# Six tiles of three blocks in a second network, and a last expert in ranges of 384 and 256 rows

## The chip, the core and the metric

The kernel runs on one core of one Trainium2 chip. Times are device microseconds (us) of one execution. The clock of TensorE, as the profile grants it, has two levels here, 2.4 and 1.2 GHz. Engines are named as in the profile: PE is TensorE (PEld its weight loads), DVE VectorE, ACT ScalarE, POOL GpSimd, SP SyncE; a q behind a name is the engine's DMA queue.

## The reference, cut to what matters

Windowed attention gives 2304 rows of 512; each row goes to two of eight experts (512 to 1024 to 512), and the weighted sum of their two answers goes through a second network (512 to 2048 to 512).

```python
x = attention(q, k, v)                                   # 2304 x 512
...
for e in range(8):                                       # each row has two experts
    h = np.maximum(x[mask] @ w1[e], 0.0)
    out[mask] += top2_w[mask, k, None] * (h @ w2[e])
...
h = x @ w_in                                             # 512 -> 2048
g = h * np.clip(h + 3.0, 0.0, 6.0) / 6.0
return g @ w_out                                         # 2048 -> 512
```

## The kernel before

Every product is made of three matmuls in a reduced 32-bit type: weights and rows are each split into a high and a low half (names beginning with h and l), and high by high, high by low, low by high are summed in PSUM.

**The experts.** Each expert has room for five blocks of 128 rows (`CAP`). It works in two ranges. For experts 1 to 7 each range takes 320 rows in its first product (`expert_sub`, lines 898 to 912): eight f blocks, each 12 matmuls with the rows as the moving operand, then a ReLU on ScalarE into `hh` and the low half on VectorE into `hl`. An f block's sum lies in one of four PSUM tiles in turn (three `ph`, one `ph4`), so f block 4 takes the tile that `hl` of f block 0 reads last. The second product (lines 913 to 933) makes the output blocks m, 24 matmuls of 512 columns each: m 0 and 1 behind the first range, m 2 to 4 behind the second. ScalarE copies a block to `y` and stores it in the DRAM tensor `y_rows`.

**The second network.** Its 18 blocks of 128 rows come in tiles (`TILES`, line 944). To begin a tile, each of its blocks is gathered from `y_rows` by eight indirect DMAs of GpSimd into two tiles `xg` (`fetch`), combined with the gates on ScalarE and VectorE, four instructions each (`combine`), and transposed and split into `xh` and `xl` (`tokens`). A gather of block i of tile 0 has to wait for block i of every expert, the last one's too. A tile does two halves, each with eight f blocks of 12 matmuls, whose moving width is the tile's rows (256 for two blocks, 384 for three), and 24 matmuls of 512 columns for each block of rows.

**What sets the order.** From the experts on, every engine runs its instructions in the order in which the code is written. Side work is hung into the loops by keys: `put(f, "f", 3, 0)` runs f inside f block 3 (ahead of its ReLU), `("f", 3, 1)` behind it, `("m", 2, 1)` inside output block 2. Beside the gathers these are the steps that fetch and split the second network's weights: a copy of the high half on ScalarE (line 589), the low half on VectorE (line 595), through two buffers `wraw`. Before the change tile 0's two blocks are gathered in the last expert's second range and combined behind its f blocks, at its output blocks 2 and 3.

Of the kernel before, what the change touches and what calls it, by code (L numbers as in the profile page):

```python
# [21 lines left out]
E = 8  # L22
# [7 lines left out]
CAP = 5  # L30
LIM = CAP * 128
SUBS = ((0, 2), (2, CAP))

HOLD = SUBS[0][1] * 128
KNOWN = 2

# [9 lines left out]
def attention_moe_kernel(ctx, tc, q, k, v, w_gate, w_noise, noise, w1, w2, w_in, w_out, out):  # L46
# [459 lines left out]
    XG, XT2 = {}, {}  # L506
# [31 lines left out]
    def turn_rows(src, hi, lo, c0):  # L538

        tr = ps.tile([128, 4, 128], F32, name="tr", bufs=2)  # L540
        for a in range(4):
            pe.transpose(tr[:, a], src[:, a * 128:(a + 1) * 128], ident)
        halves(tr, hi, lo, c0)

    def columns(e, s):
        if (e, s) not in XT2:
            XT2[e, s] = [(ep if s else mp).tile([128, 4, 384], F32R, name=f"{nm}{s}") for nm in ("xh", "xl")]
        return XT2[e, s]

    def build(e, m):  # L550
        if e == 0:
            s = int(m >= SUBS[0][1])
            turn_rows(XG[e, m], *columns(e, s), 128 * (m - SUBS[s][0]))
        elif m == 2:

            turn(XG[e, m], (*columns(e, 0), 0), (*columns(e, 1), 0))
        else:
            s = int(m > 2)
            turn(XG[e, m], (*columns(e, s), 64 + 128 * (m - 3 * s)))
# [319 lines left out]

    def expert_sub(e, s, at):  # L880

        m0, m1 = SUBS[s]


        if e == 0:
            n, c0, b0 = 128 * (m1 - m0), 0, 0
        else:
            n, c0, b0 = 64 * CAP, 64 * s, 64 - 64 * s
        xh, xl = XT2[e, s]
        if e == 0 or s == 0:  # L890
            HH[:] = [[ep.tile([128, 384], F32R, name=f"{nm}{f}") for f in range(8)] for nm in ("hh", "hl")]
        hh, hl = HH

        def also(*key):
            for f in at.get(key, ()):
                f()

        for f in range(8):
            p = sums()[:, :n]
            fs = slice(128 * f, 128 * f + 128)  # L900
            for d in range(4):
                wh, wl = W["w1", e, d]
                pe.matmul(p, wh[:, fs], xh[:, d, :n], start=(d == 0), stop=False)  # L903
                pe.matmul(p, wh[:, fs], xl[:, d, :n], start=False, stop=False)  # L904
                pe.matmul(p, wl[:, fs], xh[:, d, :n], start=False, stop=(d == 3))  # L905
                if d == 1:
                    also("f", f, 0)
                also("d", f, d)
            cs = slice(c0, c0 + n)
            act.activation(hh[f][:, cs], p, AF.Relu)  # L910
            dve.scalar_tensor_tensor(hl[f][:, cs], p, 0.0, hh[f].bitcast(F32)[:, cs], op0=OP.max, op1=OP.subtract)  # L911
            also("f", f, 1)
        for m in range(m0, m1):
            also("m", m, 0)
            ms = slice(b0 + 128 * (m - m0), b0 + 128 * (m - m0) + 128)
            if e and m % 3 == 2:
                p = ps.tile([128, DM], F32, name="tr", bufs=2)
            else:
                p = eps.tile([128, DM], F32, name="py", bufs=2)
            for f in range(8):  # L920
                wh, wl = W["w2", e, f // 2]
                ws = slice(512 * (f % 2), 512 * (f % 2) + 512)
                pe.matmul(p, hh[f][:, ms], wh[:, ws], start=(f == 0), stop=False)  # L923
                pe.matmul(p, hh[f][:, ms], wl[:, ws], start=False, stop=False)  # L924
                pe.matmul(p, hl[f][:, ms], wh[:, ws], start=False, stop=(f == 7))  # L925
                if f in (2, 5):
                    also("m", m, 1 + f // 3)
                also("s", m, f)
            also("m", m, 3)
            y = ep.tile([128, DM], F32, name="y")  # L930
            act.copy(y.rearrange("q (a k y) -> q k a y", a=4, k=4), p.rearrange("q (k a y) -> q k a y", a=4, k=4))  # L931
            r = (m * E + e) * 128
            act.dma_start(ybuf[r:r + 128], y)
# [7 lines left out]
               [Narrow(w_out, w_out32, c) for c in range(PER // CH)], 2)  # L941
    A1, M = SUBS[0][1], CAP

    TILES = (2, 3, 3, 3, 3, 2, 2)
    BASES = [sum(TILES[:t]) for t in range(len(TILES))]
    TT = 128 * max(TILES)
    NF = F2 // 128
# [26 lines left out]
    for e in range(E):  # L974
        at = {}

        def put(f, *key):
            at.setdefault(key, []).append(f)
# [27 lines left out]
        if 0 < e < 5:  # L1006
            for f in range(8):
                put(lambda: next(table, None), "f", f, 1)
        expert_sub(e, 0, at)

        at.clear()
# [14 lines left out]
        if e + 1 < E:  # L1026
            for m, f, late in ((0, 0, ("f", 6, 0)), (1, 2, ("m", A1, 1)), (2, 4, ("m", A1 + 1, 0))):
                put(lambda m=m: gather(e + 1, m), "f", f, 0)
                put(lambda m=m: build(e + 1, m), *late)
            if e == 0:  # L1030
                for key in (("f", 1, 1), ("f", 3, 0), ("f", 4, 1), ("f", 6, 1), ("m", A1, 1), ("m", A1, 3),
                            ("m", A1 + 1, 2), ("m", A1 + 2, 1)):
                    put(wq.settle, *key)
            for key in ((("f", 1, 0), ("f", 2, 1), ("f", 4, 0), ("f", 5, 1), ("f", 7, 1), ("m", A1, 2),
                         ("m", A1 + 1, 1), ("m", A1 + 1, 3)) if e == 0 else
                        (("f", 1, 1), ("f", 5, 0), ("m", A1, 0), ("m", A1 + 1, 1), ("m", A1 + 2, 0))):
                put(wq.step, *key)
            if e:
                for key in (("f", 0, 1), ("f", 2, 1), ("f", 4, 1), ("m", A1, 2), ("m", A1 + 1, 2), ("m", A1 + 2, 2)):
                    put(nq.step, *key)  # L1040
        else:
            while nq.at < len(nq.items):
                nq.step()
            store_narrow()
            narrow.close()
            wpool[2] = pool_of(ctx, "w2")
            fp = pool_of(ctx, "ffn")
            for f in (1, 3, 6):
                put(wq.step, "f", f, 1)
            for i in range(2):  # L1050
                put(lambda i=i: fetch(0, i), "f", 3 * i, 0)
                put(lambda i=i: combine(0, i), "m", A1 + i, i)
                put(lambda i=i: tokens(0, i), "m", A1 + i, 1 + i)
            for key in (("m", A1, 2), ("m", A1 + 1, 0), ("m", A1 + 2, 0), ("m", A1 + 2, 2)):
                put(wq.step, *key)
            for key in (("f", 2, 1), ("f", 4, 1), ("f", 7, 1), ("m", A1, 3), ("m", A1 + 1, 3), ("m", A1 + 2, 1), ("m", A1 + 2, 3)):
                put(wq.settle, *key)
            put(lambda: fetch(1, 0), "m", A1 + 2, 0)
        expert_sub(e, 1, at)
        store_narrow()  # L1060

# [100 lines left out]
    for t, ni in enumerate(TILES):  # L1162
# [9 lines left out]

        if t + 1 < len(TILES):

            put(lambda: fetch(t + 1, 1), "f", 2)
            put(lambda: combine(t + 1, 0), 0, 0, 3)
            put(lambda: tokens(t + 1, 0), 0, 1, 0)
            if TILES[t + 1] > 2:
                put(lambda: fetch(t + 1, 2), 0, 1, 1)
            put(lambda: combine(t + 1, 1), 0, 1, 3)  # L1180
            put(lambda: tokens(t + 1, 1), 1, 0, 0)
            if TILES[t + 1] > 2:
                put(lambda: combine(t + 1, 2), 1, 0, 3)
                put(lambda: tokens(t + 1, 2), 1, 1, 0)
            if 0 < t < len(TILES) - 2:
                put(lambda: fetch(t + 2, 0), 1, 1, 3)
        if t == 0:
            for key in (("f", 2), ("f", 6), (0, 0, 1), (0, 0, 6)):
# [5 lines left out]
        for half in range(2):  # L1194
# [18 lines left out]
            for i in range(ni):  # L1213
                if t + 1 == len(TILES) and half == 1 and i == 1:
                    e = mybir.EngineType
                    tc.mark_branch_hint_location("over", "LikelyTaken", engines=[e.PE, e.DVE, e.SP])
                ms = slice(128 * i, 128 * i + 128)
                if half == 0:
                    py[i] = eps.tile([128, DM], F32, name="py", bufs=2) if i < 2 else ps.tile([128, DM], F32, name="tr", bufs=2)
                for f in fs:  # L1220
                    wh, wl = W["w_out", f // 2]
                    ws = slice(512 * (f % 2), 512 * (f % 2) + 512)
                    pe.matmul(py[i], gh[f][:, ms], wh[:, ws], start=(f == 0), stop=False)  # L1223
                    pe.matmul(py[i], gh[f][:, ms], wl[:, ws], start=False, stop=False)  # L1224
                    pe.matmul(py[i], gl[f][:, ms], wh[:, ws], start=False, stop=(f == NF - 1))  # L1225
                    also(half, i, f % 8)
                if half == 1:

                    if t == 0 and i == 1:
                        fetch(2, 0)  # L1230
                    store(py[i], 128 * (BASES[t] + i))
    overflow()

# [31 lines left out]
```

## Time and profile before

| | us |
|---|---|
| median of 3 runs | 1007.03 |
| lowest, highest | 1004.6, 1007.49 |
| the profiled execution's own time | 1009.37 |
| its span, first to last instruction | 1007.6 |
| TensorE busy in it | 983.8 |
| VectorE, ScalarE, GpSimd busy | 573.9, 467.8, 324.7 |

The span is what the trace covers; 1.8 us of the profiled execution's time lie around it. TensorE's matmuls are pipelined: a row's duration is longer than the spacing of two rows, and the spacing is what a matmul costs in a row of them.

### The profile page before, as it was taken

What the parts mean: (1) busy time and instruction counts of PE and PEld (TensorE: products, weight loads), DVE (VectorE), ACT (ScalarE), POOL (GpSimd) and SP (SyncE); (2) the same over time, 40 slices, a digit from 0 to 9 for tenths busy, and PEclk for the clock granted to TensorE, in tenths of its full rate; (3) what the DMA queues carried; (4) which work ended last, traced back from release to release, by engine and by line L of the source; (5) the groups of instructions that cost most, each with busy time, mean ns of one, the idle gap of its engine ahead of it and who ended that gap; (6) DMA issues with size and microseconds to landing.
All of it is one profiled execution on the core that took longest, in us unless ns stands there. A gap on an engine that the chain in (4) does not pass through costs nothing.

```text
span 1007.6 us, 17479 instructions
## 1 busy us (share of the span) xinstructions
PE 983.8 (98%) x6392; PEld 893.7 (89%) x6392; DVE 573.9 (57%) x1550; ACT 467.8 (46%) x1032; POOL 324.7 (32%) x351
## 2 busy tenths in 40 slices
PE   8989898999999999999999999999999999999998
PEld 7979886999897999999998988989988998899997
DVE  6687975556777776666667656444333433344322
ACT  6867651444544454444454546434333433334333
POOL 2122202732535334242431276732343234410000
PEclk9999998999999999999999999999999999999999
DMA  9897441546656666656666454200111002000000
GB/s 168 169 221 190 119 147 50 165 139 201 214 163 197 192 184 193 186 186 209 215 195 196 151 191 133 70 23 19 58 32 46 24 26 63 27 27 22 11 11 23
DMA packets 116395, 122.43 MB, mean 122 GB/s; under 512 B 69840, under 2 KB 78288, under 8 KB 116304
## 3 DMA queue, kind: packets, MB, share of 16 engines
q1 hardware_dynamic: 96144, 86.17, 31.0%
q0 software_dynamic: 9488, 19.94, 7.1%
q10 hardware_dynamic: 10672, 15.15, 4.1%
q8 instruction: 51, 0.84, 0.3%
q14 instruction: 40, 0.33, 0.1%
HBM read 92.91 MB, written 28.31 MB: 120 GB/s over the span
## 4 chain that ended last, share of the span: by engine, by line
PE 80%; DVE 9%; DMA 5%; ACT 3%; issue 2%; POOL 0%; ACTq 0%; DVEq 0%; SPq 0%
PE ph L1204 6%; PE ph L1202 6%; PE ph L1203 6%; PE ph L903 6%; PE ph L904 6%; PE ph L905 6%; PE py L1225 5%; PE py L1224 5%; PE py L1223 5%; PE py L923 4%; PE py L924 4%; PE py L925 4%; PE s L242 3%; PE pv L295 2%; PE tr L1225 1%
## 5 line engine op out<-in xcount | busy, mean ns | idle before, releaser
L522 POOL DMA_INDIRECT xg<-x_rows,idx x140 | 145.1, 1037 | 221.2 <-DVE xt L533 169.8
L959 POOL DMA_INDIRECT xg<-y_rows,rows x144 | 144.3, 1002 | 222.4 <-DVE xg L967 74.5
L1207 DVE SCALAR_TENSOR_TENSOR g<-g,ph 128x384 f32<-128x384 f32 (+1 forms) x112 | 55.7, 497 | 158.8 <-ACT g L1206 154.5
L1206 ACT ACTIVATE g<-ph,three 128x384 f32<-128x384 f32 (+1 forms) x112 | 60.0, 536 | 100.7 <-PE ph L1204 97.7
L911 DVE SCALAR_TENSOR_TENSOR hl<-ph,hh 128x320 fp32r<-128x320 f32 (+2 forms) x128 | 61.0, 487 | 74.1 <-ACT hh L910 74.1
L1212 DVE TENSOR_TENSOR hl<-g,hh 128x384 fp32r<-128x384 f32 (+1 forms) x112 | 56.2, 502 | 58.9 <-ACT hh L1210 56.1
L910 ACT ACTIVATE hh<-ph 128x320 fp32r<-128x320 f32 (+2 forms) x128 | 54.6, 436 | 65.2 <-PE ph L905 61.2
L1210 ACT CAST hh<-g 128x384 fp32r<-128x384 f32 (+1 forms) x112 | 52.4, 467 | 63.8 <-DVE g L1207 63.8
L527 ACT CAST xh<-xt 128x512 fp32r<-128x512 f32 (+1 forms) x60 | 33.6, 570 | 81.9 <-DVE xt L533 81.2
L528 DVE TENSOR_TENSOR xl<-xt,xh 128x512 fp32r<-128x512 f32 (+1 forms) x60 | 37.2, 630 | 39.7 <-ACT xh L527 39.7
L242 PE MATMUL s<-kt,qbd 128*128 128x128 f32 x288 | 43.7, 293 | 0.2 <-ACT kt L227 0.2
L242 PEld LDWEIGHTS s<-kt,qbd 128*128 128x128 f32 x288 | 40.2, 207 | 0.6 <-ACT kt L227 0.5
L157 POOL TENSOR_SCALAR vt<-vt 64x520 f32<-64x520 f32 (+1 forms) x32 | 19.3, 604 | 57.0 <-DMA vt<-in_v_dram 53.2
L533 DVE STREAM_TRANSPOSE xt<-xg 128x512 f32<-128x512 f32 x53 | 37.4, 706 | 0.4
L762 DVE SCALAR_TENSOR_TENSOR na<-mag,raw 128x256 f32<-128x256 f32 x64 | 26.9, 420 | 12.7 <-DMA w_out<-na 5.1
L759 ACT ACTIVATE mag<-raw 128x256 f32<-128x256 f32 x64 | 27.6, 431 | 12.6 <-DVE na L768 12.6
L257 ACT ACTIVATE pb<-sm,mx 128x128 f32<-128x128 f32 x90 | 30.0, 397 | 5.8 <-DVE mx L250 5.7
L768 DVE CUSTOM_DVE_ANT_0 na<-mag,nr 128x512 uint16<-128x512 uint16 x64 | 27.3, 426 | 9.5 <-DVE mag L767 0.5
L931 ACT COPY y<-py 128x512 f32<-128x512 f32 x33 | 19.3, 584 | 27.1 <-PE py L925 14.1
L270 ACT COPY ptb<-pt 128x384 f32<-128x384 f32 x48 | 23.1, 480 | 12.7 <-PE pt L265 10.7
L767 DVE SCALAR_TENSOR_TENSOR mag<-na,mag 128x256 int32<-128x256 int32 x64 | 27.2, 425 | 2.2
L295 PE MATMUL pv<-vt,ptb 128*64 128x65 f32 x640 | 26.1, 226 | 1.8 <-DVE xbuf L314 1.8
(520 smaller groups left out, 3201.7 us busy)
## 6 DMA issues: line engine op xcount, KB each, us to landing
wraw<-in_moe_w_dram SPq DMA_DIRECT2D x60, 512.0 KB, 4.6
y_rows<-y ACTq DMA_DIRECT2D x40, 256.0 KB, 3.4
raw<-in_moe_w_in_dram SPq DMA_DIRECT2D x32, 256.0 KB, 3.8
raw<-in_moe_w_out_dram SPq DMA_DIRECT2D x32, 256.0 KB, 3.0
rq<-in_q_dram SPq DMA_DIRECT2D x32, 144.0 KB, 3.7
rk<-in_k_dram SPq DMA_DIRECT2D x32, 144.0 KB, 2.9
x_rows<-xbuf SPq DMA_DIRECT2D x18, 256.0 KB
out_dram<-y ACTq DMA_DIRECT2D x17, 256.0 KB, 2.2
```

The costliest lines, as they stand in the source:

```text
L242: pe.matmul(s[:, i, :], l, KT[n][:, k0:k0 + 128], start=(g in LIGHT), stop=(g in LIGHT or i == 2))
L522: pool.indirect_dma_start(out=t[:, i], out_offset=None, in_=pieces(xrows), in_offset=bass.IndirectOffsetOnAxis(ap=idx4[:, i, e, m:m + 1], ...
L903: pe.matmul(p, wh[:, fs], xh[:, d, :n], start=(d == 0), stop=False)
L904: pe.matmul(p, wh[:, fs], xl[:, d, :n], start=False, stop=False)
L905: pe.matmul(p, wl[:, fs], xh[:, d, :n], start=False, stop=(d == 3))
L911: dve.scalar_tensor_tensor(hl[f][:, cs], p, 0.0, hh[f].bitcast(F32)[:, cs], op0=OP.max, op1=OP.subtract)
L959: pool.indirect_dma_start(out=g[:, r], out_offset=None, in_=pieces(left), in_offset=bass.IndirectOffsetOnAxis(ap=rows4[:, r, tt, j:j + 1], ...
L1202: pe.matmul(p, wh[:, c], xh[:, d, :n], start=(d == 0), stop=False)
L1203: pe.matmul(p, wh[:, c], xl[:, d, :n], start=False, stop=False)
L1204: pe.matmul(p, wl[:, c], xh[:, d, :n], start=False, stop=(d == 3))
L1206: act.activation(g, p, AF.Relu, bias=three)
L1225: pe.matmul(py[i], gl[f][:, ms], wh[:, ws], start=False, stop=(f == NF - 1))
```

## The change

The second network takes six tiles of three blocks instead of tiles of 2, 3, 3, 3, 3, 2 and 2. So that tile 0's third block can be gathered, the last expert's ranges become 384 rows (blocks 0 to 2, the third one whole) and 256 rows (blocks 3 and 4), its `hh` and `hl` are new tiles in its second range, and output block 2 is made behind the first range. Gathers, combines and weight steps get new places.

```diff
+LAST = ((0, 3), (3, CAP))
...
+        elif e + 1 == E:
+            s = int(m >= LAST[0][1])
+            turn(XG[e, m], (*columns(e, s), 128 * (m - LAST[s][0])))
...
-        m0, m1 = SUBS[s]
...
-        if e == 0:
+        m0, m1 = (LAST if e + 1 == E else SUBS)[s]
...
+        if e in (0, E - 1):
             n, c0, b0 = 128 * (m1 - m0), 0, 0
...
-    TILES = (2, 3, 3, 3, 3, 2, 2)
+    TILES = (3,) * 6
...
+        if e + 1 == E:
+            put(lambda: fetch(0, 0), "m", 1, 2)
+            put(lambda: fetch(0, 1), "m", 2, 2)
         expert_sub(e, 0, at)
...
-            for i in range(2):
-                put(lambda i=i: fetch(0, i), "f", 3 * i, 0)
-                put(lambda i=i: combine(0, i), "m", A1 + i, i)
-                put(lambda i=i: tokens(0, i), "m", A1 + i, 1 + i)
...
+            for i, (c, k) in enumerate(((("f", 0, 0), ("f", 1, 0)), (("f", 3, 0), ("f", 4, 0)),
+                                        (("m", 3, 1), ("m", 3, 2)))):
+                put(lambda i=i: combine(0, i), *c)
+                put(lambda i=i: tokens(0, i), *k)
+            put(lambda: fetch(0, 2), "f", 2, 0)
+            put(lambda: fetch(1, 0), "m", 4, 2)
...
-            if 0 < t < len(TILES) - 2:
+            if t < len(TILES) - 2:
                 put(lambda: fetch(t + 2, 0), 1, 1, 3)
...
-                    if t == 0 and i == 1:
-                        fetch(2, 0)
```

VectorE's rows before the change, in the last expert's second range from f block 4 to tile 0's block 0 (L911 makes `hl`, L595 a low weight half, L967 is the combine of a block, its `xg` operands the two gathered tiles):

```order
L911 SCALAR_TENSOR_TENSOR hl4_7265<-ph_7633,hh4_7257 128x320
L595 TENSOR_TENSOR lzb_7631<-wraw_7582,hzb_7630 128x1024
L911 SCALAR_TENSOR_TENSOR hl5_7266<-ph_7649,hh5_7258 128x320
L911 SCALAR_TENSOR_TENSOR hl6_7267<-ph_7664,hh6_7259 128x320
L911 SCALAR_TENSOR_TENSOR hl7_7268<-ph4_7684,hh7_7260 128x320
L595 TENSOR_TENSOR lva_7682<-wraw_7628,hva_7681 128x1024
L967 SCALAR_TENSOR_TENSOR xg_7548<-xg_7553,gates4_110,xg_7548 128x128 x4
```

The same engine in the changed kernel, from the start of that range (lines are four further down: L915 makes `hl`, L971 combines, L534 and L529 are the transpose and the low half of `tokens`):

```order
L971 SCALAR_TENSOR_TENSOR xg_7516<-xg_7521,gates4_110,xg_7516 128x128 x4
L915 SCALAR_TENSOR_TENSOR hl0_7595<-ph_7603,hh0_7587 128x256
L534 STREAM_TRANSPOSE xt_7635<-xg_7516 128x4x4x32
L529 TENSOR_TENSOR xl0_7634<-xt_7635,xh0_7633 128x4x128
L915 SCALAR_TENSOR_TENSOR hl1_7596<-ph_7626,hh1_7588 128x256
L599 TENSOR_TENSOR lxb_7536<-wraw_7492,hxb_7535 128x1024
L915 SCALAR_TENSOR_TENSOR hl2_7597<-ph_7653,hh2_7589 128x256
L599 TENSOR_TENSOR lyb_7651<-wraw_7533,hyb_7650 128x1024
L971 SCALAR_TENSOR_TENSOR xg_7560<-xg_7565,gates4_110,xg_7560 128x128 x4
L915 SCALAR_TENSOR_TENSOR hl3_7598<-ph4_7679,hh3_7590 128x256
```

The combines of tile 0's blocks 0 and 1 have moved from behind hl7 to ahead of hl0 and of hl3.

GpSimd's rows in the changed kernel behind the last expert's own gathers (six tiles `xg` for tile 0, four gathers into each):

```order
L963 DMA xg_7516<-y_rows,rows4_109 128x128 x4
L963 DMA xg_7521<-y_rows,rows4_109 128x128 x4
L963 DMA xg_7560<-y_rows,rows4_109 128x128 x4
L963 DMA xg_7565<-y_rows,rows4_109 128x128 x4
L963 DMA xg_7660<-y_rows,rows4_109 128x128 x4
L963 DMA xg_7665<-y_rows,rows4_109 128x128 x4
```

Before, the fifth and sixth of these belonged to tile 1; the order and number of the gathers is the same, only whose block they are has moved.

## Rows read from the trace of the kernel before

**Rows 1.** page, part 1, and TensorE's clock from part 2 (40 slices, tenths)

```profile
PE 983.8 (98%) x6392; PEld 893.7 (89%) x6392; DVE 573.9 (57%) x1550; ACT 467.8 (46%) x1032; POOL 324.7 (32%) x351
PEclk9999998999999999999999999999999999999999
```

**Rows 2.** TensorE's timeline, tile 6: start us, us, instruction; first of each stretch

```profile
957.74 0.28 PE L1202 MATMUL ph<-xh,hsa 128*128 128x256 f32 x1
...
969.25 0.40 PE L1223 MATMUL py<-hwa,hh 128*128 128x512 f32 x1
...
980.16 0.28 PE L1202 MATMUL ph<-xh,hxb 128*128 128x256 f32 x1
```

**Rows 3.** TensorE's timeline, last expert's range 1, and a half of tile 4

```profile
546.91 0.30 PE L903 MATMUL ph<-xh,hwa 128*128 128x320 f32 x1
...
560.99 0.39 PE L923 MATMUL py<-hsb,hh 128*128 128x512 f32 x1
...
879.87 0.33 PE L1202 MATMUL ph<-xh,hxb 128*128 128x384 f32 x1
...
896.54 0.39 PE L1223 MATMUL py<-hsb,hh 128*128 128x512 f32 x1
```

**Rows 4.** TensorE's timeline, tile 0; in brackets the idle time before, and its releaser

```profile
602.32 0.28 PE L1202 MATMUL ph<-xh,hsa 128*128 128x256 f32 x1
...
619.44 0.50 PE L1223 MATMUL py<-hza,hh 128*128 128x512 f32 x1 [0.53 <-ACT hh L1210]
...
626.27 0.28 PE L1202 MATMUL ph<-xh,hxb 128*128 128x256 f32 x1
```

**Rows 5.** GpSimd's timeline: first and last of sixteen gathers, and the next

```profile
572.60 0.99 POOL L959 DMA_INDIRECT xg<-y_rows,rows  x1 [34.62 <-DVE mag L767]
...
592.23 1.81 POOL L959 DMA_INDIRECT xg<-y_rows,rows  x1 [0.30 <-issue]
596.19 0.94 POOL L959 DMA_INDIRECT xg<-y_rows,rows  x1 [2.16 <-DMA y_rows<-y]
```

**Rows 6.** VectorE's timeline at block 1 of tile 0, and ScalarE's cast

```profile
597.32 0.35 DVE L967 SCALAR_TENSOR_TENSOR xg<-xg,gates 128x128 f32<-128x128 f32 x1 [1.97 <-DMA xg<-y_rows,rows]
597.71 0.71 DVE L533 STREAM_TRANSPOSE xt<-xg 128x512 f32<-128x512 f32 x1
599.11 0.69 DVE L528 TENSOR_TENSOR xl<-xt,xh 128x512 fp32r<-128x512 f32 x1 [0.69 <-ACT xh L527]
598.45 0.62 ACT L527 CAST xh<-xt 128x512 fp32r<-128x512 f32 x1 [3.39 <-DVE xt L533]
```

**Rows 7.** ScalarE's timeline ahead of the last expert's store of block 0

```profile
565.97 1.05 ACT L589 CAST hua<-wraw 128x1024 fp32r<-128x1024 f32 x1 [4.13 <-DMA wraw<-w_in]
568.11 0.56 ACT L931 COPY y<-py 128x512 f32<-128x512 f32 x1
568.70 0.33 ACTq L933 DMA_DIRECT2D y_rows<-y  x1
```

**Rows 8.** gathers of the second network (tile xg, from 560 us): ns min/median/max

```profile
L959 POOL DMA_INDIRECT xg<-y_rows,rows x144: 938/944/1977, 572.6 to 903.7; - x144
...
DMA to landing us min/median/max: 2.4/2.5/4.8
```

**Rows 9.** page, part 5: hl of the experts

```profile
L911 DVE SCALAR_TENSOR_TENSOR hl<-ph,hh 128x320 fp32r<-128x320 f32 (+2 forms) x128 | 61.0, 487 | 74.1 <-ACT hh L910 74.1
```

**Rows 10.** a wait on TensorE; two stretches: busy by engine, PEclk, DMA share, GB/s

```profile
104.92 0.17 PE L403 MATMUL g<-mk,before 128*128 128x8 f16 x1 [2.73 <-DVE mk L394]
105.00:110.00 5.00, 5.00 (x48) 4.87 (x49) 4.83 (x25) 2.00 (x6) 1.14 (x2) 0.66 0.01 2
155.00:160.00 5.00, 4.89 (x42) 4.59 (x42) 3.97 (x23) 0.59 (x2) 0.00 (x0) 0.50 0.01 3
```

**Rows 11.** TensorE's last matmul; page, part 6: stores of the output

```profile
1002.35 0.39 PE L1225 MATMUL py<-hvb,hl 128*128 128x512 f32 x1
out_dram<-y ACTq DMA_DIRECT2D x17, 256.0 KB, 2.2
```

More of the change, by code (lines that the diff above doesn't have):

```diff
@@ L889, in expert_sub @@
         xh, xl = XT2[e, s]
-        if e == 0 or s == 0:
+        if e in (0, E - 1) or s == 0:
             HH[:] = [[ep.tile([128, 384], F32R, name=f"{nm}{f}") for f in range(8)] for nm in ("hh", "hl")]
@@ L1049, in attention_moe_kernel @@
                 put(wq.step, "f", f, 1)
-            for i in range(2):
-                put(lambda i=i: fetch(0, i), "f", 3 * i, 0)
-                put(lambda i=i: combine(0, i), "m", A1 + i, i)
-                put(lambda i=i: tokens(0, i), "m", A1 + i, 1 + i)
-            for key in (("m", A1, 2), ("m", A1 + 1, 0), ("m", A1 + 2, 0), ("m", A1 + 2, 2)):
+            for i, (c, k) in enumerate(((("f", 0, 0), ("f", 1, 0)), (("f", 3, 0), ("f", 4, 0)),
[4 more added lines that the diff above has]
+            put(lambda: fetch(1, 0), "m", 4, 2)
+            for key in (("m", 3, 0), ("m", 3, 3), ("m", 4, 1), ("m", 4, 3)):
                 put(wq.step, *key)
-            for key in (("f", 2, 1), ("f", 4, 1), ("f", 7, 1), ("m", A1, 3), ("m", A1 + 1, 3), ("m", A1 + 2, 1), ("m", A1 + 2, 3)):
+            for key in (("f", 2, 1), ("f", 4, 1), ("f", 7, 1), ("m", 3, 2), ("m", 4, 0), ("m", 4, 2)):
                 put(wq.settle, *key)
-            put(lambda: fetch(1, 0), "m", A1 + 2, 0)
         expert_sub(e, 1, at)
```

## The prediction

> **What bounds the kernel now.** I read the page first: TensorE is busy for 983.8 of 1007.6 us, at full clock in nearly every slice [rows 1]. So the time is what TensorE's instructions take one behind the other, plus its few waits. The chain of work that ended last says the same, so I left it and read TensorE's own timeline, one row for each matmul, taking the first row of each stretch: the difference of two such rows over the matmuls between is the spacing. 96 matmuls of 256 columns take 969.25 − 957.74 = 11.51 us, 119.9 ns each; the 48 of 512 behind them 10.91 us, 227.3 ns [rows 2]. 96 of 384 columns take 16.67 us, 173.6 ns; 96 of 320, the last expert's, 14.08 us, 146.7 ns [rows 3]. From tile 1 on every stretch repeats these numbers to 0.02 us. Only tile 0 of the second network differs: its first half runs from 602.32 to 626.27, 23.95 us where 11.51 + 10.91 = 22.42 would do. The 1.53 us are waits for the late hh and hl of its last f blocks [rows 4].
>
> Then I read what feeds tile 0, engine by engine, around the last expert (546.91 to 602.32). GpSimd issues one gather after another, sixteen from 572.60 to 592.23, so 19.63/15 = 1.31 us apart, and is held before the first for the landing of expert 7's store of block 0, issued at 568.70; the row names a VectorE instruction, but the next one that waits, at 596.19, names the store of a block, and 3.9 us from issue to the first gather is what a store takes [rows 5, 7].
>
> **What the change does to TensorE.** Seven tiles become six. Each f block has 12 matmuls, a tile 192. Three tiles of 256 columns cost 3 × 2 × 11.51 = 69.06 us; the two of 384 in their place 2 × 2 × 16.67 = 66.68. The 512-column matmuls are as many as before (18 blocks). That is −2.4 us. The last expert trades 2 × 14.08 for 16.67 + 11.51: +0.02 us, nothing. The rows price a matmul by its columns plus 12.5 ns (2 × 119.9 − 227.3), and 192 fewer of those are the 2.4 us [rows 2]. The Trainium skill (TensorE: Matmul & The Clock Gate, section Back-to-back issue gap) has a spacing of N/2.4 ns plus about 2.5 ns, which is an estimate of 109 ns for 256 columns where the row has 119.9. By that page the removed instructions would be worth only 192 × 2.5 ns = 0.5 us, and the sum below 1.9 us worse; the measured rows decide here.
>
> **What it moves.** Tile 0 now needs three blocks before it starts instead of two, so 24 gathers instead of 16, and its first two blocks are combined in the last expert's second range in among the f blocks, no longer behind them. On VectorE the four combine instructions now stand ahead of hl0 and of hl3. The engines run their rows in order, so hl0 waits for block 0's second gather tile and hl3 for block 1's. The f blocks have four PSUM tiles: f4 needs the one that hl0 reads, f7 the one that hl3 reads. Before, these combines stood behind hl7, where a late gather stops VectorE (1.97 us at 597.32) but not TensorE [rows 6].
>
> The times, each step from rows. Range 1 of the last expert starts at 546.91 as before. It takes 16.67 + 3 × 5.45 = 33.02 us, so range 2 starts at 579.93 and unhindered its f blocks would start every 1.44 us: f4 at 585.7, f7 at 590.0, tile 0 at 602.35.
>
> The first gather: before, the store of block 0 was held up on ScalarE by the copy of a weight half that waited 4.13 us for its load, and that load is issued behind a conversion that stands after f6. Copy at 565.97, y copied at 568.11, stored at 568.70, first gather 572.60 [rows 5, 7]. This chain hangs on f6, which now ends 7 × (2.084 − 1.760) = 2.3 us later. So the first gather is at 574.9. Its lower bound is a copy right behind TensorE's block 0 (569.2), and the same 4.5 us from copy to gather: 573.7.
>
> Gather to landing is 2.5 us in the median, 4.8 at most [rows 8]. Block 0's last gather is issued at 574.9 + 7 × 1.31 = 584.1 and lands at 586.6. The last combine (0.35) and hl0 (0.49 at 320 columns) [rows 6, 9] put f4 at 587.4, 1.7 us late. f5 waits for hl1, which stands behind the transpose, the two casts of block 0 (0.71 + 0.62 + 0.69) and itself: 589.9, another 1.0 late. f6 is about 0.2 late behind a weight half. Block 1's last gather is issued at 574.9 + 15 × 1.31 = 594.6 and lands at 597.1; combine and hl3 put f7 at 597.9, where f6 would have let it start at 592.9. All together f7 is 597.9 − 590.0 = 7.9 us late. **+7.9 us**; from below 5.8 (first gather 573.7, gathers 1.24 us apart, the median 0.94 and 0.30 between [rows 5, 8], landing 2.5), from above 10.2 (landing 4.8, as the row at 597.32 had it).
>
> Block 2 is gathered last: 574.9 + 23 × 1.31 + 2.5 = 607.5, plus combine, transpose and the two casts (0.35 + 0.71 + 0.62 + 0.69) and their hand-overs, 610.1. Tile 0 can start at 597.9 + 1.44 + 10.91 = 610.3, so this cover is thin but holds: nothing in the sum, 2.2 us if that landing takes 4.8.
>
> The clock: an idle TensorE loses it. After 2.73 us of waiting before 104.92 the next 5 us show 0.66; a later stretch shows 0.50 for all of its 5 us [rows 10]. The levels are 2.4 and 1.2 GHz, so these are 3.4 and 5 us at the lower one, and 1.7 and 2.5 us lost. The 5.0 us before f7 are longer than the first of these waits. I take **+1.7**, bounds 0 and 2.5. What is lost at f4 to f6 costs nothing, since f7 waits anyway.
>
> Tile 0's own 1.53 us of waits: the 384-column blocks give ScalarE and VectorE 2.08 instead of 1.44 us for each f, but the weight halves they convert there come later by what was lost. I take them as they were, **0**, bounds −1.5 and +1.5. Tile 0 still takes two steps of 33 us each, so tile 1's 24 gathers (31 us) are covered; without that cover their excess would be added. The stores are hidden as before. At the end the hint for the last branch now stands a block earlier; 5.3 us follow the last matmul's start at 1002.35, of which 2.2 are a store's landing [rows 11]. I charge nothing for it, with the other 3.1 us as the upper bound.
>
> **Sum:** −2.4 + 7.9 + 1.7 + 0 = +7.2 us on the profiled execution's 1009.37 us (1007.6 of span). That execution is 2.3 us above the median of the runs, 1007.03, so for a median I say 1007.0 + 7.2 = 1014.2, rounded to 1014.
>
> **Rivals.** First, faster: the waits are absorbed, as in before, and only the columns and tile 0's waits remain, −2.4 − 1.5, about 1003. For this hl3 must be done when f7 is due, at 590.0, so block 1 must land by 589.1. From a first gather at 574.9 that asks for gathers (589.1 − 2.5 − 574.9)/15 = 0.78 us apart, and the shortest gather of 144 is 0.94 without the 0.30 between [rows 5, 8]. Chance 0.08, for something that I misread in the order. Second, a half effect: gathers start early, land fast, the clock stays: −2.4 + 5.8 − 1.5 = +1.9, about 1009, within 0.3% of before. Chance 0.07. Third, block 2 becomes the bound: its landing takes 4.8, tile 0 starts at 612.4 or later, and with the clock's loss and late weight halves the sum goes to +10 or +12, 1017 to 1019. For it speaks that the gather issued at 592.23 took 1.81 us and was waited for until 597.32 [rows 5, 6]; against it that TensorE's own lateness with the clock's 1.7 covers most. Chance 0.07. Fourth, the columns save less than the rows say: if only 0.5 us comes back, +9.1, 1016. Chance 0.03, as every stretch shows 119.9. It is the case of the page above.
>
> **How the numbers follow.** The forecast has 0.75. About 0.3%, 3 us, is what a measurement of this kernel can tell from no change. Slower by more: 0.75 + 0.07 + 0.03 = 0.85; within: 0.07; faster: 0.08. The extremes of the terms give +1.9 to +15 (−2.4 + 10.2 + 2.5 + 1.5 + 3.1 at the upper end); all bad ends together are unlikely, so 1008 to 1019 holds the forecast's own spread, half of the third rival and half of the second, about 0.8.
>
> **What would show it.** In the changed profile: the f blocks of the 256-column range of expert 7 stretch from 11.5 to about 19 us, with two waits of TensorE for hl on VectorE, the longer before f7; VectorE waits for gathers ahead of hl3; a slice at reduced clock right behind; 24 gathers in one row; first halves of 16.67 us in six tiles. The prediction is wrong if gathers begin before 573 or stand under 1 us apart, or if f4 and f7 start without a wait. With range 2 right and the sum off, look at the clock and at tile 0's start.

## The result, and the profile after

The changed kernel takes 1015.11 us (median of 6 runs, 1012.98 to 1018.96), the kernel before, in runs on the same chip, 1006.02 (6 runs, 1004.6 to 1007.49). The ratio is 1.0083, 95% interval 1.0066 to 1.0101: slower by 0.8%.

The profiled execution took 1014.1 us, its span is 1012.3. Profiled spans of kernels with the same work up to the last expert differ in when that expert begins, from 540.2 to 549.4 us over the eleven kernels here, and no matmul of the change stands ahead of it. So I compare from the first matmul of the last expert's range 1 to the end of the span: 1007.6 − 546.91 = 460.7 us before [rows 3], 1012.3 − 542.80 = 469.5 now, +8.8. Taking a common event as zero is the first thing to do with two such traces.

TensorE's timeline of the changed kernel, the first row of each stretch and the rows with a wait:

```profile
542.80 0.33 PE L907 MATMUL ph<-xh,hwa 128*128 128x384 f32 x1
...
575.82 0.28 PE L907 MATMUL ph<-xh,hwa 128*128 128x256 f32 x1
...
583.62 0.39 PE L907 MATMUL ph<-xh,hwa 128*128 128x256 f32 x1 [1.88 <-DVE hl L915]
585.95 0.39 PE L907 MATMUL ph<-xh,hwa 128*128 128x256 f32 x1 [0.64 <-DVE hl L915]
...
594.52 0.58 PE L907 MATMUL ph<-xh,hwa 128*128 128x256 f32 x1 [5.39 <-DVE hl L915]
...
597.24 0.63 PE L927 MATMUL py<-hsb,hh 128*128 128x512 f32 x1
...
609.15 0.33 PE L1210 MATMUL ph<-xh,hsa 128*128 128x384 f32 x1
...
626.03 0.39 PE L1231 MATMUL py<-hwa,hh 128*128 128x512 f32 x1
...
644.08 0.33 PE L1210 MATMUL ph<-xh,hxb 128*128 128x384 f32 x1
...
1007.15 0.39 PE L1233 MATMUL tr<-hvb,hl 128*128 128x512 f32 x1
```

Range 1 takes 33.02 us, as its matmuls must. Range 2's f blocks take 597.24 − 575.82 = 21.42 us instead of 11.51, with waits at f4, f5 and f7. Seven f blocks of 1.44 us put f7 at 585.89; it starts at 594.52, **8.63 us late**. From there f7 and the 48 matmuls of 512 columns take 609.15 − 594.52 = 14.63 us, where 1.44 + 10.91 would do: **2.28 us**. The windows there name the clock (columns: busy time and instructions of each engine, granted clock, DMA share, GB/s):

```profile
590.00:592.50 2.50, 0.00 (x0) 0.00 (x0) 0.35 (x1) 1.04 (x1) 1.89 (x3) 1.00 0.80 292
592.50:595.00 2.50, 0.48 (x2) 0.49 (x3) 1.75 (x5) 0.00 (x0) 1.89 (x3) 0.51 0.23 59
595.00:597.50 2.50, 2.50 (x13) 2.50 (x13) 1.82 (x4) 2.39 (x6) 1.97 (x2) 0.50 0.23 57
597.50:600.00 2.50, 2.50 (x8) 1.93 (x8) 2.50 (x5) 0.36 (x1) 2.12 (x2) 0.62 0.44 107
600.00:602.50 2.50, 2.50 (x13) 2.06 (x12) 0.05 (x1) 0.76 (x1) 1.89 (x3) 1.00 0.87 302
```

In the wait the clock falls to its lower level, 1.2 GHz (0.50), and is back behind 600. Tile 0's first half takes 644.08 − 609.15 = 34.93 us instead of 33.03: 1.90 us of waits, 1.53 before [rows 4], so +0.37. The two 384-column tiles give back 2.38, and the last expert's two ranges cost 0.02 more; 5.15 us follow the last matmul's start, 5.25 before [rows 11]. Sum: 8.63 + 2.28 + 0.37 + 0.02 − 2.38 − 0.10 = +8.8.

VectorE at the wait for f7 and at block 2's low half, and GpSimd's gathers, first, 16th, 24th and the next:

```profile
591.53 0.35 DVE L971 SCALAR_TENSOR_TENSOR xg<-xg,gates 128x128 f32<-128x128 f32 x1 [3.04 <-DMA xg<-y_rows,rows]
593.25 0.88 DVE L971 SCALAR_TENSOR_TENSOR xg<-xg,gates 128x128 f32<-128x128 f32 x3 [1.37 <-DMA xg<-y_rows,rows]
594.04 0.42 DVE L915 SCALAR_TENSOR_TENSOR hl<-ph,hh 128x256 fp32r<-128x256 f32 x1
...
606.91 0.69 DVE L529 TENSOR_TENSOR xl<-xt,xh 128x512 fp32r<-128x512 f32 x1 [0.69 <-ACT xh L528]
```

```profile
571.37 1.16 POOL L963 DMA_INDIRECT xg<-y_rows,rows  x1 [37.18 <-DVE na L772]
...
590.87 0.94 POOL L963 DMA_INDIRECT xg<-y_rows,rows  x1 [0.30 <-issue]
...
602.42 0.94 POOL L963 DMA_INDIRECT xg<-y_rows,rows  x1 [0.30 <-issue]
611.25 0.94 POOL L963 DMA_INDIRECT xg<-y_rows,rows  x1 [7.89 <-DMA y_rows<-y]
```

hl3 (594.04) ends in front of f7 (594.52). Ahead of it stand the combines of block 1, which wait for gathers, and the gathers come without a break from 571.37 to 602.42, 31.05/23 = 1.35 us apart. Block 2, gathered last, has its low half xl at 606.91 + 0.69 = 607.60, 1.55 us before tile 0 begins.

### The profile page after: what moved, and what is told of

Same layout as the page of the kernel before. It is cut to its first block, busy times and chain, and to the rows that moved or that the text cites. A ratio compares the mean times of both kernels' runs of the same rounds, so it can differ in the third digit from the quotient of the medians.

```text
span 1012.3 us, 16993 instructions
## 1 busy us (share of the span) xinstructions
PE 980.6 (97%) x6200; PEld 889.7 (88%) x6200; DVE 566.8 (56%) x1517; ACT 460.1 (45%) x999; POOL 322.9 (32%) x351
## 4 chain that ended last, share of the span: by engine, by line
PE 78%; DVE 9%; DMA 6%; issue 3%; ACT 3%; POOL 1%; SPq 0%; ACTq 0%; DVEq 0%; POOLq 0%
PE ph L1212 6%; PE ph L1210 6%; PE ph L1211 6%; PE ph L907 6%; PE ph L908 6%; PE ph L909 6%; PE py L927 4%; PE py L928 4%; PE py L929 4%; PE py L1233 4%; PE py L1232 4%; PE py L1231 4%; PE s L243 2%; PE tr L1232 2%; PE tr L1233 2%
## 5 line engine op out<-in xcount | busy, mean ns | idle before, releaser
L963 POOL DMA_INDIRECT xg<-y_rows,rows x144 | 142.2, 988 | 229.6 <-DVE xg L971 78.6
L1215 DVE SCALAR_TENSOR_TENSOR g<-g,ph 128x384 f32<-128x384 f32 x96 | 53.2, 554 | 163.1 <-ACT g L1214 163.1
L1214 ACT ACTIVATE g<-ph,three 128x384 f32<-128x384 f32 x96 | 55.7, 581 | 110.9 <-PE ph L1212 110.5
L915 DVE SCALAR_TENSOR_TENSOR hl<-ph,hh 128x320 fp32r<-128x320 f32 (+2 forms) x128 | 61.1, 487 | 70.5 <-ACT hh L914 70.4
L1220 DVE TENSOR_TENSOR hl<-g,hh 128x384 fp32r<-128x384 f32 x96 | 53.6, 558 | 53.9 <-ACT hh L1218 53.9
L1218 ACT CAST hh<-g 128x384 fp32r<-128x384 f32 x96 | 49.3, 514 | 60.0 <-DVE g L1215 60.0
L529 DVE TENSOR_TENSOR xl<-xt,xh 128x512 fp32r<-128x512 f32 (+1 forms) x59 | 37.2, 639 | 39.7 <-ACT xh L528 39.7
L534 DVE STREAM_TRANSPOSE xt<-xg 128x512 f32<-128x512 f32 x53 | 37.4, 706 | 0.3
L907 PE MATMUL ph<-xh,hwa 128*128 128x320 f32 (+2 forms) x80 | 25.9, 324 | 8.9 <-DVE hl L915 8.2
L971 DVE SCALAR_TENSOR_TENSOR xg<-xg,gates 128x128 f32<-128x128 f32 x72 | 21.1, 347 | 18.8 <-ACT xg L970 10.8
```

What stands on the lines that cost most here:

```text
L963: pool.indirect_dma_start(out=g[:, r], out_offset=None, in_=pieces(left), in_offset=bass.IndirectOffsetOnAxis(ap=rows4[:, r, tt, j:j + 1], ...
```

## The experiments

Three theories stood. **Order** (the prediction's step): the combines of tile 0 stand ahead of hl0 and hl3 on VectorE, so f4 and f7 wait. **Gather rate**: 24 gathers behind block 0's store fill GpSimd until 602, and tile 0 needs the last of them, wherever the combines stand; the order only chooses the place of the wait. **Split**: the 384 + 256 ranges and the weight steps that stand closer together cost it. All times are medians; each kernel ran beside the kernel before on its chip. The last column is the time from range 1's start to the end of the span.

| kernel | us | before | ratio, 95% interval | from range 1 |
|---|---|---|---|---|
| before | | | | 460.7 |
| changed | 1015.11 | 1006.02 | 1.0083 (1.0066 to 1.0101) | 469.5 |
| combines behind the f blocks | 1016.14 | 1005.32 | 1.0096 (1.0069 to 1.0122) | 470.4 |
| half the gathers | 1006.60 | 1005.32 | 1.0015 (0.9997 to 1.0032) | 461.6 |
| ranges alone | 1008.65 | 1005.32 | 1.0030 (1.0014 to 1.0045) | 463.5 |
| TensorE kept busy | 1014.98 | 1005.32 | 1.0096 (1.0070 to 1.0122) | 469.6 |
| store sooner | 1014.86 | 1005.73 | 1.0094 (1.0072 to 1.0115) | 469.7 |
| whole rows | 1004.38 | 1005.73 | 0.9981 (0.9968 to 0.9994) | 460.0 |
| before, whole rows | 1006.44 | 1005.73 | 1.0000 (0.9984 to 1.0015) | 460.0 |
| whole rows, old order | 1006.43 | 1006.86 | 0.9995 (0.9981 to 1.0009) | 461.0 |
| whole rows, no wait | 1003.97 | 1006.86 | 0.9976 (0.9963 to 0.9988) | 458.3 |

**Combines behind the f blocks.** The order alone is undone.

```diff
-            for i, (c, k) in enumerate(((("f", 0, 0), ("f", 1, 0)), (("f", 3, 0), ("f", 4, 0)),
-                                        (("m", 3, 1), ("m", 3, 2)))):
+            for i, (c, k) in enumerate(((("f", 7, 1), ("m", 3, 0)), (("m", 3, 2), ("m", 4, 0)),
+                                        (("m", 4, 2), ("m", 4, 3)))):
...
-            put(lambda: fetch(0, 2), "f", 2, 0)
-            put(lambda: fetch(1, 0), "m", 4, 2)
+            put(lambda: fetch(0, 2), "m", 3, 1)
+            put(lambda: fetch(1, 0), "m", 4, 3)
```

> The changed kernel, with the combine and the transpose of tile 0's three blocks hung behind the last expert's f blocks of the second range, at its output blocks 3 and 4; gathers at the same rate. Theory order (mine: the combines stand ahead of hl0 and hl3 on VectorE and a PSUM tile is not read in time): f4 and f7 start without a wait, the 256-column stretch takes 11.5 to 12 us instead of 21.42, and if tile 0 then starts without a new wait the time is about 1004. Rival gather rate (24 gathers at 1.30 us from about 571.4 end at 602, land at 604 to 605, and need combine, transpose and casts, wherever they stand): the wait moves to the start of tile 0, which would be due at about 598 and can't start before 607 to 609; tile 0 starts where it starts in the changed kernel, the time stays at 1014 to 1015. Rival split (the 384 + 256 ranges and the weight steps that stand closer together are what costs): no change, and the f blocks still wait.

No gain. The f blocks of range 2 now run in 11.5 us, and the waits of TensorE from the last expert to tile 1 shrink to one, at the start of tile 0:

```profile
PE ph L1210 <- ACT xh L528: 10.6, 1, 10.6
```

```profile
604.24 0.94 POOL L963 DMA_INDIRECT xg<-y_rows,rows  x1 [0.30 <-issue]
605.49 0.94 POOL L963 DMA_INDIRECT xg<-y_rows,rows  x1 [0.30 <-issue]
```

```profile
608.05 0.35 DVE L971 SCALAR_TENSOR_TENSOR xg<-xg,gates 128x128 f32<-128x128 f32 x1 [0.96 <-DMA xg<-y_rows,rows]
608.32 1.22 DVE L599 TENSOR_TENSOR lya<-wraw,hya 128x1024 fp32r<-128x1024 f32 x1
609.45 0.70 DVE L534 STREAM_TRANSPOSE xt<-xg 128x512 f32<-128x512 f32 x1
```

GpSimd's 24th gather is issued at 605.49, VectorE's last combine ends at 608.4, and TensorE begins tile 0 at 610.86, 66.20 us behind range 1's start (544.66); in the changed kernel it is 609.15 − 542.80 = 66.35. The wait has moved and kept its size. That is gather rate, against order. The loss of clock has moved with it: the granted clock is 0.50 from 604 to 616, and tile 0's first f blocks take 630.50 − 610.86 = 19.64 us instead of 16.67. The gathers aren't the bound to the last microsecond: the train was slower here (32.17/23 = 1.40 us apart), and a weight half of 1.22 us stands ahead of the transpose.

**Half the gathers.** Tile 0 takes the first expert's rows twice, which leaves the second expert's term out of its 384 rows; 12 gathers, same places.

```diff
-        for j in range(2):
+        for j in range(1 if t == 0 else 2):
...
-        y0, y1 = Y[t, i, 0], Y[t, i, 1]
+        y0, y1 = Y[t, i, 0], Y[t, i, min(1, t)]
```

> The changed kernel, but tile 0 gathers only the rows of each token's first expert, 12 gathers instead of 24, and adds them twice; this leaves the second expert's term out of tile 0's three blocks. Nothing else moves: the combines stand where they stood, ahead of hl0 and hl3. Theories order and gather rate alike: block 0's last gather is issued 4 x 1.30 = 5.2 us sooner and block 1's 8 x 1.30 = 10.4 us sooner, so f7 no longer waits and f4 hardly; 9 to 12 us less than the changed kernel, 1003 to 1006. Theory split: the gathers don't matter, it stays at 1014 to 1015.

The loss falls from 9.1 us to 1.3, with the order as it was; one wait of an f block is left, 0.29 us. It ends a little above the range that I gave, since tile 0 now waits for the late weight halves (1.27 us for g, 1.1 us for hh and hl, as in the changed kernel).

**Ranges alone.** The split, its gathers and weight steps, with the old seven tiles.

```diff
-    TILES = (3,) * 6
+    TILES = (2, 3, 3, 3, 3, 2, 2)
...
+            for i, (c, k) in enumerate(((("m", 3, 0), ("m", 3, 1)), (("m", 4, 0), ("m", 4, 1)))):
```

> Only one part of the change: the last expert in 384 + 256 rows, gathers in its first range, and weight steps as in the changed kernel, but the second network in the tiles of before (2, 3, 3, 3, 3, 2, 2), with tile 0's two blocks combined behind the f blocks. Theories order and gather rate: the f blocks of the second range run in 11.5 to 12 us; 16 gathers from about 571.4 end at 591 and are covered until 602; tile 0's own waits may grow by the compressed weight steps; 1007 to 1011. Theory split: the whole loss is here already, plus the 2.4 us that the columns give back are missing: 1015 to 1018.

+3.3 us, a third of the loss. The place is not the f blocks (11.51 us) but the start of tile 0. GpSimd's first gather, TensorE's wait, and ScalarE and VectorE at the combine of tile 0's last block:

```profile
577.25 0.94 POOL L963 DMA_INDIRECT xg<-y_rows,rows  x1 [36.55 <-DVE mag L771]
```

```profile
607.08 0.39 PE L1208 MATMUL ph<-xh,hsa 128*128 128x256 f32 x1 [2.05 <-ACT xh L528]
```

```profile
601.02 1.05 ACT L593 CAST hxa<-wraw 128x1024 fp32r<-128x1024 f32 x1 [1.37 <-DMA wraw<-w_out]
...
602.96 1.28 ACT L970 ACTIVATE xg<-xg,gates 128x128 f32<-128x128 f32 x4 [0.40 <-ACT y L935]
```

```profile
603.39 1.23 DVE L971 SCALAR_TENSOR_TENSOR xg<-xg,gates 128x128 f32<-128x128 f32 x4 [1.88 <-ACT xg L970]
```

Its range 1 starts at 549.42, so GpSimd's first gather comes 27.83 us behind it, 2.14 later than before (25.69), and tile 0 starts 57.66 us behind it, 2.25 later than before (55.41) [rows 3 to 5]. The two delays are alike, but the gathers don't hold tile 0 here: VectorE's four combine instructions wait for ScalarE and none of them for a gather. ScalarE comes to its part of the combine only behind the weight half hxa, which waited for its load, and the copy of an output block. So this third of the loss is split's: it is the weight steps, with the place that I gave this combine behind one of them. The whole-row kernels further down keep the ranges and the weight steps and lose nothing to them, so this run doesn't say how much of the changed kernel's own loss they hold.

**TensorE kept busy.** This takes out the clock term alone.

```diff
+            if e + 1 == E and s == 1 and f == 7:
+                idle = ps.tile([128, 512], F32, name="tr", bufs=2)
+                for _ in range(80):
+                    pe.matmul(idle[:, 0:128], ones, ones, start=True, stop=True)
```

> The changed kernel with 80 extra 128-column fp16 matmuls into a spare PSUM tile between f6 and f7 of the last expert's second range, where TensorE waits 5.4 us. They take about 80 x 55 to 107 ns = 4.4 to 8.6 us, so they fill most of the wait and may overrun it by some 2 us at the lower clock. If the half clock behind the wait is a cost of its own (mine: 2.3 us in the trace, f7 and the 48 matmuls of 512 columns behind it), the stretch of 512 columns behind the f blocks takes 10.9 instead of 11.9 us, and the time is 1 to 2.3 us less than the changed kernel, 1013 to 1014. If the clock there costs nothing that something else would not take anyway (gathers of block 2 bound the start of tile 0), the stretch shortens but tile 0 waits as long, and the time stays.

The clock stayed at 2.4 GHz (1.00 in every window from 585 to 607.5), and the time did not move. TensorE's timeline (the 80 take 4.64 us, 58 ns each), and the window in which the changed kernel had 0.50:

```profile
588.44 4.64 PE L906 MATMUL tr<-ones 128*128 128x128 f16 x80
594.56 0.38 PE L911 MATMUL ph<-xh,hwa 128*128 128x256 f32 x1 [1.48 <-DVE hl L919]
...
617.11 0.44 PE L1214 MATMUL ph<-xh,hsa 128*128 128x384 f32 x1 [1.37 <-DVE g L1219]
```

```profile
595.00:597.50 2.50, 2.50 (x18) 2.24 (x17) 1.81 (x4) 2.34 (x6) 1.89 (x3) 1.00 0.18 52
```

From f7 to tile 0 it takes 12.44 us instead of 14.63, so the clock did cost 2.2 there; f7 comes 0.65 later behind range 2's start, and tile 0 starts 64.8 us behind range 1 instead of 66.35. There a new wait takes it back: tile 0's first f blocks go to 18.57 us instead of 16.88. ScalarE's row for the cause, in this kernel:

```profile
612.67 1.05 ACT L593 CAST hya<-wraw 128x1024 fp32r<-128x1024 f32 x1 [4.69 <-DMA wraw<-w_out]
613.96 1.05 ACT L593 CAST hza<-wraw 128x1024 fp32r<-128x1024 f32 x1 [0.23 <-DMA wraw<-w_out]
614.91 0.58 ACT L939 COPY y<-py 128x512 f32<-128x512 f32 x1
615.52 0.33 ACTq L941 DMA_DIRECT2D y_rows<-y  x1
615.89 0.58 ACT L1218 ACTIVATE g<-ph,three 128x384 f32<-128x384 f32 x1 [0.40 <-PE ph L1216]
```

Two weight halves wait for their loads ahead of the activation of tile 0's first f block. The loads' own queue names what they wait for:

```profile
SPq L585 <- DVE lwa L599: 7.9, 1, 7.9
```

VectorE makes lwa at 607.19, behind the combine and the split of block 2 that it waited for. So behind the late gathers a second chain of nearly the same length ends at tile 0.

**Store sooner.** Weight steps out of the way of block 0's copy.

```diff
-            for key in (("f", 3, 1), ("m", 0, 0), ("m", 1, 1), ("m", 1, 3)):
+            for key in ((("f", 3, 1), ("m", 1, 0), ("m", 1, 3), ("m", 2, 1)) if e + 1 == E else
+                        (("f", 3, 1), ("m", 0, 0), ("m", 1, 1), ("m", 1, 3))):
```

> The changed kernel with three weight steps of the last expert's first output blocks put a block later, so that ScalarE's copy of block 0 no longer stands behind a weight half that waits for its load. The first gather comes 1.5 to 1.9 us sooner, about 26.8 instead of 28.6 us behind the start of range 1. If the train of gathers sets the end of the wait (as the kernel with the combines moved behind the f blocks showed), f7 is due the same 1.5 to 1.9 us sooner and the time is 1.5 to 2 us less than the changed kernel, 1013; if the late weight halves take it back at tile 0, it stays at 1014 to 1015.

A miss. ScalarE copies block 0 as soon as TensorE has it, 22.35 us behind range 1's start (541.42) instead of 23.11, which is all that there was to gain, 0.76. And the first gather comes 5.46 us behind the store's issue instead of 4.86. The load of a weight half now goes out at 564.25 and runs beside the store; that it is the cause is likely but not shown, since the same time is 4.0 to 4.9 us in the other kernels with this split. GpSimd's first gather comes 28.43 us behind range 1's start instead of 28.57, and the time is the same.

```profile
563.77 0.59 ACT L935 COPY y<-py 128x512 f32<-128x512 f32 x1 [2.46 <-PE py L929]
564.39 0.33 ACTq L937 DMA_DIRECT2D y_rows<-y  x1
```

**Whole rows.** If the number of gathers binds, fewer and larger ones must free it. Tile 0's blocks are gathered as rows of 512 and transposed on TensorE, and the combines are put in f3, behind f7 and behind output block 3. The control is the kernel before with the same for its two blocks (`WHOLE = (0, 1)`).

```diff
+    WHOLE = (0, 1, 2)
...
+            if t == 0 and i in WHOLE:
+                g = Y[t, i, j] = mp.tile([128, DM], F32, name="xg", bufs=4)
+                pool.indirect_dma_start(out=g, out_offset=None, in_=left,
+                                        in_offset=bass.IndirectOffsetOnAxis(ap=rows1[:, tt, j:j + 1], axis=0))
+                continue
...
+            tr = ps.tile([128, 4, 128], F32, name="tr", bufs=2)
+            for k in range(4):
+                pe.transpose(tr[:, k], s[:, k], ident)
+            halves(tr, *XT2[t], 128 * i)
```

> The changed kernel, with tile 0's three blocks gathered in whole rows of 512: 6 gathers of 256 KB instead of 24 of 64 KB (expert 0's gathers of this size take 0.96 us each where the small ones take 0.94), their transposes on TensorE instead of VectorE (12 matmuls, about 0.45 us a block), and the combines spread behind f3, f7 and output block 3. Theory gather rate: the six gathers are bound by the stores of blocks 1 and 2 alone; nothing of tile 0 is late, no f block waits. Against the changed kernel 8.6 + 2.3 us of waits and clock go and 1.3 us of transposes come: about 1005, level with the kernel before; with tile 0's own 1.9 us of waits gone too, 1003 to 1004. If 256 KB land so late (over 8 us) that tile 0 still waits, 1008 to 1012.

> The kernel before, with tile 0's two blocks gathered in whole rows (4 gathers instead of 16) and transposed on TensorE. It is the control to the kernel of six tiles with whole rows: without the waits of either, six tiles should be 2.4 us less of matmuls and one block's transposes (0.45 us) more. Against the kernel before: +0.9 us of transposes, and up to 1.5 us less of tile 0's own waits if these come from late gathers; -0.6 to +0.9, no change that can be measured.

The first falls to 1004.38, below the kernel before; TensorE's only waits in the stretch are 0.52 and 0.96 us for two combines ahead of the transposes. The control stays where the kernel before is, so whole rows alone bring the old tiles nothing that can be measured: they pay where the gathers bind.

**Whole rows with the old order, and without the two waits.** The first takes the changed kernel's own combine places back (f0, f3 and output block 3) with the places of its gathers, which makes four corners of order and gathers; the second moves two combines ahead and the transposes of block 0 an f block later. The corners aren't exact: the kernel with whole rows still has block 0's combine ahead of hl3, where the kernel with the combines behind has all three behind the f blocks. Against the kernel with whole rows:

```diff
-            for i, (c, k) in enumerate(((("f", 3, 0), ("f", 5, 0)), (("f", 7, 1), ("m", 3, 2)),
-                                        (("m", 3, 3), ("m", 4, 1)))):
...
+            for i, (c, k) in enumerate(((("f", 0, 0), ("f", 2, 0)), (("f", 3, 0), ("f", 6, 0)),
+                                         (("m", 3, 1), ("m", 4, 0)))):
...
+            for i, (c, k) in enumerate(((("f", 3, 0), ("f", 6, 0)), (("f", 7, 0), ("m", 3, 2)),
+                                         (("m", 3, 0), ("m", 4, 1)))):
```

> The changed kernel with its own combine places (f0, f3, output block 3: ahead of hl0 and hl3), but with tile 0 gathered in whole rows and transposed on TensorE. With the kernel that moved the combines alone this makes four corners: old and new order, slow and fast gathers. Theory gather rate: the order alone cost nothing beyond the train of gathers; block 0 lands 1 us and block 1 about 8.5 us into range 2, hl3 is done at 10 and f7 due at 10.1, so f7 waits 0 to 1 us and the time is 1004 to 1006. Theory order (combines ahead of hl are a loss by themselves): 5 us or more of waits for hl remain, 1010 to 1012.

> The kernel of six tiles with whole rows, with the combines of blocks 1 and 2 half an output block sooner and the transposes of block 0 an f block later, so that TensorE no longer waits for VectorE ahead of the transposes (0.52 + 0.96 us there). 1.5 us less than that kernel: 1003, about 2.5 us below the kernel before. If a combine now stands ahead of something that is due, 1004 to 1005.

With the combines ahead of hl0 and hl3 and fast gathers, no f block waits for hl; what is left is 2.6 us for the combines ahead of the transposes, which I had put too early:

```profile
PE tr L996 <- DVE xt L982: 2.6, 2, 1.6
```

The four corners, each against the kernel before on its chip: small gathers +9.1 us (changed order) and +10.8 (combines behind), whole rows −0.4 (changed order) and −1.4 (combines mostly behind). The gathers are worth 9 to 12 us; the order moves it by 1 to 2 us, once up and once down, which the intervals hardly tell from nothing. Without the two waits the kernel takes 1003.97, 0.24% (0.12 to 0.37) less than the one before; the trace lists no wait of TensorE from 560 us on. It is the fastest version here. GpSimd's six gathers in it, with the first of tile 1, and the groups by line (ns min/median/max; L971 gathers pieces, L966 whole rows; the last row is L966's landing):

```profile
568.51 1.69 POOL L966 DMA_INDIRECT xg<-y_rows,rows  x1 [37.26 <-DVE na L773]
570.50 0.94 POOL L966 DMA_INDIRECT xg<-y_rows,rows  x1 [0.30 <-issue]
576.92 0.94 POOL L966 DMA_INDIRECT xg<-y_rows,rows  x1 [5.47 <-DMA y_rows<-y]
578.16 1.95 POOL L966 DMA_INDIRECT xg<-y_rows,rows  x1 [0.30 <-DVE hl L917]
582.55 0.95 POOL L966 DMA_INDIRECT xg<-y_rows,rows  x1 [2.44 <-DVE hl L917]
583.80 0.94 POOL L966 DMA_INDIRECT xg<-y_rows,rows  x1 [0.30 <-issue]
599.32 1.29 POOL L971 DMA_INDIRECT xg<-y_rows,rows  x1 [14.58 <-ACT hya L594]
```

```profile
L971 POOL DMA_INDIRECT xg<-y_rows,rows x120: 938/944/1430, 599.3 to 891.3; - x120
```

```profile
L966 POOL DMA_INDIRECT xg<-y_rows,rows x6: 942/946/1947, 568.5 to 583.8; - x6
...
DMA to landing us min/median/max: 4.8/5.4/6.0
```

The train ends 44.5 us behind range 1's start (540.20) instead of 60.6. The second pair of gathers waits for the store of its block. The third waits for VectorE: its row names hl, the instruction behind the combine of block 0, whose four parts end at 581.81. By the code the six tiles `xg` share four buffers, and this combine reads the two that the third pair takes.

## Why the prediction was right, point by point

- **Columns, −2.4.** Right: every half from tile 0's second on shows 16.66 to 16.67 and 16.36 us, as in [rows 3]. In the fastest version, with nothing waiting, six tiles are 458.3 us where the control with seven is 460.0: 1.7 less, with one block's transposes (0.35 us) more, so about 2.1 for the columns. The Trainium skill (TensorE: Matmul & The Clock Gate, section Back-to-back issue gap) gives N/2.4 + 2.5 ns as the gap of a single matmul by itself, not of matmuls that each load their weights, as these do [rows 1]. Taken as a spacing it would have made this term 0.5 us; the rows decide against it here, 119.9 ns at 256 columns.
- **f4 and f7 late, +7.9.** Measured 8.63. First gather 28.57 us behind range 1's start, predicted 28.0; block 1's last gather 48.07, predicted 47.7. The working was right in its order, and in the first gather two errors went against each other, which was luck: the store was issued 1.92 us later than before (23.71 us behind range 1's start, 21.79 before) and not 2.3, and from its issue to the gather it took 4.86 us and not 3.9. The lower bound, 5.8, comes out at 5.6 from its own rows. What the step says of the cause is half right: the combines ahead of hl decide that f4 and f7 wait, but taking them away gives nothing, as the kernel with the combines behind shows.
- **Block 2's cover, "thin but holds".** It held, and this sentence was the more important one. Block 2 was ready 1.55 us before tile 0 began, so of the 10.9 us by which tile 0 was late the f blocks alone answer for 1.55 at the most, and the gathers for the rest. The prediction had both chains (610.1 and 610.3) and put the whole loss on the first. Right for the sum, wrong for anyone who would mend the kernel from it.
- **Clock, +1.7.** Measured 2.28, within the bounds; at full clock 2.2 of it came back and was taken again at tile 0 by the weight halves.
- **Tile 0's own waits, 0.** Measured +0.37. **The tail, 0.** Measured −0.10.
- **Rivals.** The faster one asked for gathers 0.78 us apart; they came 1.35 apart. With three quarters of the gather instructions gone, in another kernel, something near it is reached: the version without waits takes 0.24% less than the kernel before, where this rival had 0.4%.
- **The signs.** By the letter one sign of being wrong came true: the gathers begin at 571.37, before 573. The limit was meant for a range 1 that starts at 546.91, which puts it 26.1 us behind that start; the first gather comes 28.57 behind its own.

Not settled: in the whole-row kernels the transposes also leave VectorE and the scaling is one ScalarE instruction instead of four. That the number of gathers does it, and not these, rests on the kernel with half the gathers, whose combines, transposes and order are the changed kernel's. That kernel also moves half the bytes; the whole-row kernels move all of them, and no f block waits for hl in them either.

## What to carry to other kernels

When a change makes a consumer need more of a slow producer before it starts, add up the producer's train to its last item, and compare it with the start of the consumer, before looking at which instruction waits: here the order of the waiting engine set only where the wait showed. An idle stretch that is moved to another place is worth nothing; undo the order in one kernel and speed the producer up in another, and the four corners tell the two apart. That two things are late by the same amount doesn't make one the cause of the other: in the kernel with the ranges alone only the row of the waiting combine told the gathers from the weight steps. When a train of small transfers binds, look for a larger form of the same transfer and for another engine for the rearrangement that the small form paid for. The Trainium skill has the general rule (DMA: Bandwidth & Descriptors, section Rules for kernel authors): many small transfers are coalesced into one large. The rows here agree for GpSimd's time: the shortest gather of either size takes 0.94 us.

## What the runs showed that I had not expected

- A gather of 256 KB holds GpSimd hardly longer than one of 64 KB: 0.94 us at the least for both, and a median of the six of 946, 948 and 1278 ns in the three kernels that gather tile 0 so, where the small ones have 944. What grows is the landing, from a median of 2.5 us to 5.4 in the fastest version.
- Four transposes of 128 x 128 between other matmuls cost TensorE 0.35 us a block; I had estimated 0.45.
- A TensorE fed with small 16-bit matmuls kept 2.4 GHz (granted clock 1.00) through the wait in which it otherwise fell to 1.2 (0.50).
- A store issued 0.74 us sooner brought its gather only 0.14 us sooner: from its issue to the gather it took 0.6 us longer, perhaps for the weight half's load beside it.
